# Attention into experts: another order for the last two tiles and the last gate, and the loads of expert 0's rows ahead of the next raw weights

## The chip, the cores and the metric

The kernel runs on one core of one Trainium2 chip. The metric is the device time of one execution in microseconds, here the median of three runs. Beside the timed runs there is one profiled execution, from which all rows of the trace come.

## The reference

Three stages follow one another, all in float32:

```
# 1. attention with a decaying state, per batch (4) and head (8), 768 steps, 48 wide
y[t]  = r[t] @ (state + outer(u*k[t], v[t]));  state = w[t][:,None]*state + outer(k[t], v[t])
# 2. a mixture of 8 experts on x of 3072 x 384: every token goes to its best expert alone
logits = x @ w_gate;  e = argmax(logits);  gate_w = softmax(logits)[e]
eom    = sigmoid(x @ w_output_gate)[e]
out[token] = gate_w * eom * (relu(x @ w1[e]) @ w2[e])        # 384 -> 1024 -> 384
# 3. a dense block on all tokens, 384 -> 2048 -> 384
h = x @ w_in;  out = (h * clip(h + 3, 0, 6) / 6) @ w_out
```

## The kernel before

**Attention.** The 3072 tokens are 24 tiles of 128 tokens (`NT`; tile i is chunk i // 4 of batch i % 4). The loop over i (line 692) loads tile i + 4, prepares tile i + 2 on VectorE, ScalarE and GpSimd, and does the matmuls of tile i on TensorE. Steps that the change moves are small functions, each of which issues to several engines in one go:

- `scores_pe(i)`: 16 matmuls into the banks s0 and s1; `scores(i)`: VectorE copies the allowed half into `A`.
- `ymm(i, tag)`: the outputs of a tile on TensorE, then a copy to `ys` on ScalarE (L506).
- `small_a(i, j)`: gate logits of tile i and a diagonal of tile j on TensorE, into bank x, then a copy `lts` on ScalarE. `small_p(lts)`: a matmul that turns them, into bank y (`lp`). `small_v`: ScalarE copies them to `L` (L548). `diag(j, ..)`: GpSimd writes the diagonal into `A`.
- the gate of a group g of tiles: `gate_1` (maximum, differences), `gate_2` (one-hot `O`, the chosen output logit `ls`, counts `c1` and `cnt` per expert) on VectorE, `gate_exp` on ScalarE, `gate_pe` (ranks within the expert, on TensorE), `gate_3` (the row index `pi`, the sum of exponentials), `gate_4` (the scale `sg`).
- `rows_pe(i, tag)`: four transposes of `ys`; `rows_id(i)`: GpSimd writes the token's number beside the row; `rows_act(i)`: ScalarE scales the row by `sg` into `xs` (L655); `scatter(i)`: GpSimd's indirect DMA writes 128 rows of `xs` to the places `pi` of `x_w` in DRAM (L662).

A PSUM tag (x, y, k, s0, s1) is one bank: a step that takes it waits until the last reader of what stood there is done. The order on each engine is the program's (the schedule is manual); a step waits for the data that it reads. The last groups hold two tiles each: G is (a, b) with a = 22 and b = 23, G - 1 is (a-2, a-1), G - 2 is (a-4, a-3). From line 777 the order of the last steps is written out by hand.

**The hand-over.** `keep_busy(n, ..)` issues n dummy matmuls of bfloat16 on TensorE (L382); 4, 18, 10 and 14 of them (`TAILB`) stand around the last rank matmuls, the sum of the counts (L837) and the flag (L857). After the flag VectorE makes the last eight low parts `wlo` of expert 0's weights (`piece_lo`, L351). A raw weight chunk (768 KB, 128 x 1536 float32) has two buffers, so `load_raw((1, 0), ..)`, the first chunk of expert 1, can be issued only when the low part (2, 3) is made.

**Experts.** Each expert has a window of rows of `x_w` (400 for expert 0). `window(0)` (L892) loads it in four pieces (128, 128, 128 and 16 rows), each after all 24 scatters; `window_t0` transposes it (L924, twelve transposes), ScalarE and VectorE split it into a high and a low part (L926, L927), and `first_h` is the first 18 matmuls (L966, L967, L971). From there `mm3` issues three matmuls for each product (L931 to L933). SyncE issues all loads except the scatters, in program order.

Of the kernel before, what the change touches and what calls it, by code (L numbers as in the profile page):

```python
# [7 lines left out]
F32 = mybir.dt.float32  # L8
F32R = mybir.dt.float32r
BF16 = mybir.dt.bfloat16  # L10
I32 = mybir.dt.int32
U32 = mybir.dt.uint32
AF = mybir.ActivationFunctionType
# [7 lines left out]
C = 128  # L21
# [193 lines left out]
def kernel(  # L215
# [273 lines left out]
    def ymm(i, tag="y"):  # L489
        d = tl[i]  # L490
        v, A, rh = d["v"], d["A"], d["rh"]
        last = i < B
        yp = ps_o.tile([PP, PR, C], F32, tag=tag, name="yp")

        for p in range(PR):
            for f, m in ((0, 64), (1, D)):
                c0 = (2 * p + f) * D
                nc.tensor.matmul(out=yp[64 * f:64 * f + m, p, :], lhsT=v[:, c0:c0 + m], rhs=A[:, f, p, :],  # L498
                                 start=(p == 0), stop=(last and p == PR - 1), skip_group_check=True)
        for p in range(PR) if not last else ():  # L500
            sb = d["sb"]
            for r0 in (0, 64):
                nc.tensor.matmul(out=yp[r0:r0 + D, p, :], lhsT=sb[r0:r0 + D, p, :], rhs=rh[r0:r0 + D, p, :],  # L503
                                 start=False, stop=(p == PR - 1), skip_group_check=True)
        ys = st.tile([PP, PR, C], F32, tag="ys", name="ys", bufs=12)
        nc.scalar.activation(out=ys, in_=yp, func=AF.Copy)  # L506
        d["ys"] = ys
# [9 lines left out]
            gof[i0 + j] = (g, j)  # L517
    gd = {g: {} for g in range(len(grp))}

    def small_a(i, j):  # L520

        lt = ps_o.tile([128, C], F32, tag="x", name="lt")
        src = [(z, x) for z, x in ((0, tl[i]["ys"] if 0 <= i < NT else None), (1, tl[j]["m"] if j < NT else None)) if x is not None]
        if not src:
            return None
        for n, (z, x) in enumerate(src):
            for p in range(PR):
                nc.tensor.matmul(out=lt[32 * p:32 * p + 32, :], lhsT=wg_sb[:, z, p, :], rhs=x[:, p, :],  # L528
                                 start=(n == 0), stop=(n == len(src) - 1))
        lts = wk.tile([128, C], F32, tag="lts", name="lts")  # L530
        nc.scalar.activation(out=lts, in_=lt, func=AF.Copy)
        return lts

    def small_p(lts):

        lp = ps_o.tile([128, 24], F32, tag="y", name="lp")
        nc.tensor.matmul(out=lp, lhsT=lts, rhs=sel, start=True, stop=True)
        return lp

    def small_v(i, j, lp):  # L540
        if 0 <= i < NT:
            g, z = gof[i]
            if z == 0:
                gd[g]["L"] = sm.tile([128, 4, 24], F32, tag="L", name="L")
            lq = gd[g]["L"][:, z, :]
        else:
            lq = wk.tile([128, 24], F32, tag="lq", name="lq")
        nc.scalar.activation(out=lq, in_=lp, func=AF.Copy)  # L548
        return (j, lq) if j < NT else None

    def diag(j, lq):
        av = lq[:, 16:24].rearrange("t (f p) -> t f p", f=2)
        A = wk.tile([128, 2, PR, C], F32, tag="A", name="A", bufs=4)
        nc.gpsimd.affine_select(out=A, in_=av.unsqueeze(3).to_broadcast([128, 2, PR, C]), pattern=[[0, 2], [0, PR], [1, C]],
                                compare_op=ALU.is_equal, fill=0.0, base=0, channel_multiplier=-1)
        tl[j]["A"] = A
# [6 lines left out]
    def gate_1(g):  # L563

        V = nc.vector
        d = gd[g]
        n = grp[g][1]
        lg = d["L"][:, 0:n, 0:E]
        q = gps[g % 2]
        mx, i8 = q["mx"][:, 0:n], q["i8"].rearrange("t (j e) -> t j e", e=E)[:, 0:n]  # L570
        d["df"] = sm.tile([128, 4, E], F32, tag="df", name="df")[:, 0:n]
        d["m8"] = sm.tile([128, 4], F32, tag="m8", name="m8")[:, 0:n]
        V.tensor_reduce(out=mx, in_=lg, axis=AX.X, op=ALU.max)
        V.tensor_tensor(out=d["df"], in0=lg, in1=mx.unsqueeze(2).to_broadcast([128, n, E]), op=ALU.subtract)
        V.scalar_tensor_tensor(out=i8, in0=d["df"], scalar=0.0, in1=rev8.unsqueeze(1).to_broadcast([128, n, E]),
                               op0=ALU.is_equal, op1=ALU.mult)
        V.tensor_reduce(out=d["m8"], in_=i8, axis=AX.X, op=ALU.max)
# [16 lines left out]
    def gate_exp(g):  # L594
        d = gd[g]
        n = grp[g][1]
        d["ex"] = sm.tile([128, 4, E], F32, tag="ex", name="ex")[:, 0:n]
        d["e2"] = sm.tile([128, 4], F32, tag="e2", name="e2")[:, 0:n]
        nc.scalar.activation(out=d["ex"], in_=d["df"], func=AF.Exp)
        nc.scalar.activation(out=d["e2"], in_=d["ls"], func=AF.Exp, scale=-1.0)  # L600

    def gate_pe(g, tag="y"):

        i0, n = grp[g]
        ob = gd[g]["O"]
        rk = ps_o.tile([128, 4, E], F32, tag=tag, name="rk")
        co = cnt[g % 3]
        nc.tensor.matmul(out=rk[:, 0:n], lhsT=ones_b, rhs=co.unsqueeze(1).to_broadcast([128, n, E]), start=True, stop=False)
        nc.tensor.matmul(out=rk[:, 0:n], lhsT=tri, rhs=ob, start=False, stop=(n == 1))
        for j in range(n - 1):  # L610
            nc.tensor.matmul(out=rk[:, j + 1:n], lhsT=ones_b,
                             rhs=ob[:, j:j + 1].to_broadcast([128, n - 1 - j, E]), start=False, stop=(j == n - 2))
        gd[g]["rk"] = rk
# [14 lines left out]
    def gate_4(g):  # L628

        V = nc.vector  # L630
        d = gd[g]
        n = grp[g][1]
        sx = gps[g % 2]["sx"][:, 0:n]
        d["sg"] = sm.tile([128, 4], F32, tag="sg", name="sg", bufs=4)
        V.tensor_scalar(out=sx, in0=sx, scalar1=1e-9, scalar2=None, op0=ALU.add)
        V.scalar_tensor_tensor(out=sx, in0=d["e2"], scalar=1.0, in1=sx, op0=ALU.add, op1=ALU.mult)
        V.reciprocal(out=d["sg"][:, 0:n], in_=sx)

    def rows_pe(i, tag="x"):
        xp = ps_o.tile([128, PR, 128], F32, tag=tag, name="xp")  # L640
# [18 lines left out]
    def scatter(i):  # L659

        g, j = gof[i]
        ins = nc.gpsimd.indirect_dma_start(  # L662
            out=x_w, out_offset=bass.IndirectOffsetOnAxis(ap=gd[g]["pi"][:, j:j + 1], axis=0),
            in_=tl[i]["xs"], in_offset=None)
        apart(ins, scat)
# [106 lines left out]
    def rows_to(j, tag):  # L772
        rows_pe(j, tag)
        rows_id(j)
        rows_act(j)

    scores(a)
    while sq:
        scatter(sq.pop(0))
    ymm(a - 1)  # L780
    gate_1(G - 2)
    gate_2(G - 2)
    lts = small_a(a - 2, b)
    rows_to(a - 6, "k")
    diag(*small_v(a - 2, b, small_p(lts)))
    gate_exp(G - 2)
    scatter(a - 6)
    lts = small_a(a - 1, NT)
    gate_pe(G - 2)
    gate_3(G - 2)  # L790
    gate_4(G - 2)
    rows_to(a - 5, "k")
    scatter(a - 5)
    scores(b)
    small_v(a - 1, NT, small_p(lts))
    rows_to(a - 4, "k")
    scatter(a - 4)
    ymm(a)
    gate_1(G - 1)
    gate_2(G - 1)  # L800
    gate_exp(G - 1)
    gate_pe(G - 1, "k")
    gate_3(G - 1)
    gate_4(G - 1)
    ymm(b, "s0")
    lts = small_a(a, NT)
    rows_to(a - 3, "k")
    scatter(a - 3)
    small_v(a, NT, small_p(lts))
    rows_to(a - 2, "s1")  # L810
    scatter(a - 2)
    lts = small_a(b, NT)
    rows_to(a - 1, "k")
    small_v(b, NT, small_p(lts))
    scatter(a - 1)
    gate_1(G)
    gate_2(G)
    gate_exp(G)
    rows_pe(a, "s1")
    rows_pe(b, "k")  # L820
    keep_busy(TAILB[0], ps_o, "x")
    gate_pe(G)
    gate_3(G)
    gate_4(G)
    for j in (a, b):
        rows_id(j)
    for j in (a, b):
# [34 lines left out]
    nc.vector.tensor_scalar(out=usual, in0=flag_f, scalar1=0.0, scalar2=None, op0=ALU.is_equal)  # L862
    for q, r in los:
        piece_lo((0, q), r)
        if (q, r) == (2, 3):
            load_raw((1, 0), w12[1, 0])
    keep_busy(TAILB[3], ps_o, "x")
    ph.close()

# [16 lines left out]
    def window(e):  # L886
        t = xw_p.tile([128, 4, DM], F32, tag="xw", name="xw")
        full, rest = divmod(WINS[e], 128)
        for j0, n, q in [(j, 1, 128) for j in range(full)] + [(full, 1, rest)] if e == 0 else [(0, full, 128), (full, 1, rest)]:
            if q == 0:  # L890
                continue
            ins = nc.sync.dma_start(t[0:q, j0:j0 + n, :],  # L892
                                    x_w[e * N + 128 * j0:e * N + 128 * j0 + q * n, 0:DM].rearrange("(j p) d -> p j d", j=n))
            for q in scat:
                tc.add_manual_dep(ins.ins, q.ins.name, SYNC, reason="rows of the windows")
        xw[e] = t
# [192 lines left out]
        gs[blk, f] = (hi, lo)  # L1089

    window(0)
    window_t0()
    window(1)
    f64_prefetch()
# [185 lines left out]
```

## Time and profile before

| | |
|---|---|
| median of 3 runs | 818.94 us (818.75, 818.94, 822.12) |
| profiled execution | 813.9 us, span 812.1 us |
| mean granted TensorE clock | 0.987 |
| TensorE busy | 777.2 us, 96% of the span |
| VectorE, ScalarE, GpSimd busy | 476.7, 372.7, 152.6 us |
| DMA | 85.48 MB, mean 105 GB/s |

The span runs from the first to the last instruction on the core; what the execution takes beyond it lies around them. Times within the trace count from the span's start. A granted clock of 1.00 is TensorE's 2.4 GHz, 0.50 is 1.2 GHz. "Idle before" an instruction is the time in which its engine had nothing to run, with what ended the wait behind the arrow.

### The profile page before, as it was taken

Reading aid. Unit: us, or ns where it says so; the run is one execution under the profiler, and the core shown is the slowest. Engines: PE = TensorE matmul, PEld = TensorE weight load, DVE = VectorE, ACT = ScalarE, POOL = GpSimd, SP = SyncE. Lnnn points to the kernel's source line nnn. Section 1 sums busy time; section 2 is a strip of 40 time slices with the busy share of each in tenths; the row PEclk is TensorE's granted clock in tenths of the full one; section 3 lists DMA queues with packets and bytes.
Section 4 is the critical chain, followed back from the end, with each engine's and each line's share of the span. In section 5 each row is a group of like instructions: output and inputs, shape, how many; then the busy total and the mean of one; then the engine's idle time right before and its main releaser. Section 6 shows DMA issues by size and latency. Waiting matters only on the chain.

```text
span 812.1 us, 13820 instructions
## 1 busy us (share of the span) xinstructions
PE 777.2 (96%) x5385; PEld 695.2 (86%) x5397; DVE 476.7 (59%) x946; ACT 372.7 (46%) x794; POOL 152.6 (19%) x237
## 2 busy tenths in 40 slices
PE   6999998979999999998999999999999999999996
PEld 3777776759999989998898999999999999999995
DVE  7998999536678668778776533433433343343332
ACT  4766777414554455445544433433333333333331
POOL 5777888610000000000000020020001002002002
PEclk8999999979999999999999999999999999999998
DMA  9999773143676676674511010010001001001001
GB/s 220 309 293 232 203 222 118 70 159 142 200 188 228 178 223 224 195 163 125 187 40 40 1 40 1 0 40 1 1 1 39 1 1 40 1 0 40 1 1 43
DMA packets 31868, 85.48 MB, mean 105 GB/s; under 512 B 6521, under 2 KB 17985, under 8 KB 31793
## 3 DMA queue, kind: packets, MB, share of 16 engines
q1 hardware_dynamic: 28721, 75.05, 31.7%
q0 software_dynamic: 3072, 9.45, 3.2%
q8 instruction: 44, 0.72, 0.4%
q14 instruction: 31, 0.25, 0.1%
HBM read 67.11 MB, written 17.39 MB: 104 GB/s over the span
## 4 chain that ended last, share of the span: by engine, by line
issue 40%; PE 37%; DVE 8%; DMA 7%; POOL 3%; ACT 3%; SPq 0%; POOLq 0%; ACTq 0%; DVEq 0%
DMA raw<-in_w_dram 4%; PE hp L931 4%; PE hp L932 3%; PE hp L933 3%; POOL out_dram L1166 3%; PE yp L498 3%; DVE wlo L351 3%; PE sc L452 2%; PE yp L503 2%; PE yp L933 2%; PE yp L932 2%; PE yp L931 2%; PE lt L528 2%; PE wp L382 1%; PE op L933 1%
## 5 line engine op out<-in xcount | busy, mean ns | idle before, releaser
L1082 DVE SCALAR_TENSOR_TENSOR t<-t,hp 128x512 f32<-128x512 f32 x96 | 66.0, 688 | 160.9 <-ACT t L1081 160.8
L1166 POOL DMA_INDIRECT out_dram<-ob,ids_sb x24 | 24.7, 1030 | 612.6 <-ACT ob L1164 608.0
L1081 ACT ACTIVATE t<-hp,b 128x512 f32<-128x512 f32 x96 | 65.9, 686 | 160.8 <-PE hp L933 150.2
L931 PE MATMUL op<-whi,hhi 128*128 128x384 f32 x380 | 128.4, 338 | 0.0
L932 PE MATMUL op<-wlo,hhi 128*128 128x384 f32 x380 | 128.3, 338 | 0.0
L933 PE MATMUL op<-whi,hlo 128*128 128x384 f32 x380 | 128.1, 337 | 0.0
L932 PE MATMUL hp<-xlo,win_hi 128*128 128x512 f32 x288 | 113.8, 395 | 0.4 <-DVE xlo L1070 0.4
L931 PE MATMUL hp<-xhi,win_hi 128*128 128x512 f32 x288 | 112.7, 391 | 0.9 <-ACT xhi L1069 0.9
L933 PE MATMUL hp<-xhi,win_lo 128*128 128x512 f32 x288 | 112.8, 392 | 0.0
L1088 DVE TENSOR_TENSOR hlo<-t,hhi 128x512 fp32r<-128x512 f32 x95 | 65.8, 693 | 66.3 <-ACT hhi L1087 66.3
L1087 ACT ACTIVATE hhi<-t 128x512 fp32r<-128x512 f32 x95 | 60.0, 632 | 72.2 <-DVE t L1082 72.2
L931 PEld LDWEIGHTS op<-whi,hhi 128*128 128x128 f32 x380 | 71.3, 188 | 4.1
L932 PEld LDWEIGHTS op<-wlo,hhi 128*128 128x128 f32 x380 | 71.2, 187 | 3.7
L351 DVE TENSOR_TENSOR wlo<-raw,whi 128x384 fp32r<-128x384 f32 x144 | 74.3, 557 | 0.0
L327 ACT ACTIVATE whi<-raw 128x768 fp32r<-128x768 f32 x64 | 53.9, 842 | 40.2 <-DMA raw<-in_w_dram 24.8
L933 PEld LDWEIGHTS op<-whi,hlo 128*128 128x128 f32 x380 | 71.2, 187 | 0.1
L931 PE MATMUL yp<-hhi,whi 128*128 128x360 f32 (+6 forms) x192 | 65.1, 339 | 2.7 <-ACT yst L1115 2.7
L931 PE MATMUL hp<-xhi,whi 128*128 128x360 f32 (+6 forms) x186 | 65.0, 350 | 0.9 <-ACT xhi L910 0.9
L932 PE MATMUL yp<-hlo,whi 128*128 128x360 f32 (+6 forms) x192 | 65.1, 339 | 0.2 <-DVE hlo L953 0.2
L933 PE MATMUL yp<-hhi,wlo 128*128 128x360 f32 (+6 forms) x192 | 65.0, 339 | 0.0
L933 PEld LDWEIGHTS hp<-xhi,win_lo 128*128 128x128 f32 x288 | 54.1, 188 | 11.8
L932 PE MATMUL hp<-xlo,whi 128*128 128x360 f32 (+6 forms) x186 | 63.1, 339 | 0.9 <-DVE xlo L911 0.9
(171 smaller groups left out, 1402.5 us busy)
## 6 DMA issues: line engine op xcount, KB each, us to landing
raw<-in_w_dram SPq DMA_DIRECT2D x32, 768.0 KB
a<-in_att_dram SPq DMA_DIRECT2D x23, 675.5 KB
raw<-in_wout_dram SPq DMA_DIRECT2D x16, 384.0 KB
raw<-in_win_dram SPq DMA_DIRECT2D x16, 384.0 KB
v<-in_tok_dram SPq DMA_DIRECT2D x24, 192.0 KB
wo_d<-v SPq DMA_DIRECT2D x16, 192.0 KB
raw<-wo_d SPq DMA_DIRECT2D x4, 768.0 KB
xw<-x_w SPq DMA_DIRECT2D x4, 576.0 KB
```

The lines of the kernel that those rows point to most:

```text
L327: nc.scalar.activation(out=chunks[key][0][:, sl], in_=raws[key][:, sl], func=AF.Copy)
L351: nc.vector.tensor_tensor(out=lo[:, sl], in0=raws[key][:, sl], in1=hi[:, sl].bitcast(F32), op=ALU.subtract)
L452: nc.tensor.matmul(out=scs[hf][:, p, :], lhsT=kh[r0:r0 + D, p, :], rhs=rh[r0:r0 + D, p, :], start=True, stop=True)
L498: nc.tensor.matmul(out=yp[64 * f:64 * f + m, p, :], lhsT=v[:, c0:c0 + m], rhs=A[:, f, p, :], start=(p == 0), stop=(last and p == PR - 1), ...
L931: nc.tensor.matmul(out=out_ap, lhsT=lh, rhs=rh, start=first, stop=False)
L932: nc.tensor.matmul(out=out_ap, lhsT=lh, rhs=rl, start=False, stop=False)
L933: nc.tensor.matmul(out=out_ap, lhsT=ll, rhs=rh, start=False, stop=last)
L1081: nc.scalar.activation(out=t, in_=hp, func=AF.Relu, bias=b_3)
L1082: nc.vector.scalar_tensor_tensor(out=t, in0=t, scalar=6.0, in1=hp, op0=ALU.min, op1=ALU.mult)
L1087: nc.scalar.activation(out=hi, in_=t, func=AF.Copy)
L1088: nc.vector.tensor_tensor(out=lo, in0=t, in1=hi.bitcast(F32), op=ALU.subtract)
L1166: ins = nc.gpsimd.indirect_dma_start(out=out, out_offset=bass.IndirectOffsetOnAxis(ap=ids_sb[:, i:i + 1], axis=0), in_=ob, in_offset=None)
```

## The change

Four things are changed. The hand-written order of the last tiles is another one, with other banks: `scores_pe(b)`, `ymm(a)` and `ymm(b)` come earlier among their neighbours, `gate_pe(G - 1)` stands behind `ymm(b)`, and the scatters of a-2 and a-1 stand behind the last `small_v`. The last gate is a function of its own, `gate_last`, in which the sum of exponentials comes from the exponential's own accumulator on ScalarE, and the scale `sg` is made ahead of the index `pi` and of the counts. `load_raw((1, 0))` is issued after `window(0)` instead of in the midst of the low parts. And the second and fourth piece of `window(0)` are issued by ScalarE's queue.

```diff
-    def small_a(i, j):
+    def small_a(i, j, tag="x"):
...
-    def small_p(lts):
+    def small_p(lts, tag="y"):
...
+    def gate_last(g):
+        gate_1(g)
...
+        for j in range(n):
+            nc.scalar.activation(out=ex[:, j], in_=d["df"][:, j], func=AF.Exp, accum_out=sa[:, j:j + 1])
+        V.tensor_tensor(out=d["O"], in0=i8, in1=d["m8"].unsqueeze(2).to_broadcast([128, n, E]), op=ALU.is_equal)
+        keep_busy(TAILB[0], ps_o, "x")
+        gate_pe(g)
+        V.tensor_tensor(out=lo, in0=d["L"][:, 0:n, E:2 * E], in1=d["O"], op=ALU.mult)
+        V.tensor_reduce(out=ls, in_=lo, axis=AX.X, op=ALU.add)
+        nc.scalar.activation(out=e2, in_=ls, func=AF.Exp, scale=-1.0)
+        V.tensor_scalar(out=sx, in0=sa, scalar1=1e-9, scalar2=None, op0=ALU.add)
+        V.tensor_tensor(out=pb, in0=d["rk"][:, 0:n], in1=d["O"], op=ALU.mult)
+        V.tensor_reduce(out=pf, in_=pb, axis=AX.X, op=ALU.add)
+        V.scalar_tensor_tensor(out=sx, in0=e2, scalar=1.0, in1=sx, op0=ALU.add, op1=ALU.mult)
+        V.reciprocal(out=d["sg"][:, 0:n], in_=sx)
+        V.tensor_scalar(out=d["pi"][:, 0:n], in0=pf, scalar1=float(E * N - 1), scalar2=None, op0=ALU.min)
+        V.tensor_reduce(out=q["c1"], in_=d["O"].rearrange("p j e -> p e j"), axis=AX.X, op=ALU.add)
+        V.tensor_tensor(out=cnt[(g + 1) % 3], in0=q["c1"], in1=cnt[g % 3], op=ALU.add)
...
     ymm(a - 1)
+    lts = small_a(a - 2, b)
     gate_1(G - 2)
     gate_2(G - 2)
-    lts = small_a(a - 2, b)
-    rows_to(a - 6, "k")
-    diag(*small_v(a - 2, b, small_p(lts)))
     gate_exp(G - 2)
-    scatter(a - 6)
-    lts = small_a(a - 1, NT)
-    gate_pe(G - 2)
+    scores_pe(b)
+    lts_1 = small_a(a - 1, NT, "k")
+    diag(*small_v(a - 2, b, small_p(lts, "x")))
+    small_v(a - 1, NT, small_p(lts_1, "k"))
+    gate_pe(G - 2, "x")
     gate_3(G - 2)
     gate_4(G - 2)
-    rows_to(a - 5, "k")
+    rows_to(a - 6, "k")
+    scatter(a - 6)
+    ymm(a)
+    rows_to(a - 5, "x")
     scatter(a - 5)
     scores(b)
-    small_v(a - 1, NT, small_p(lts))
-    rows_to(a - 4, "k")
-    scatter(a - 4)
-    ymm(a)
+    lts = small_a(a, NT, "k")
     gate_1(G - 1)
     gate_2(G - 1)
     gate_exp(G - 1)
-    gate_pe(G - 1, "k")
+    rows_to(a - 4, "x")
+    scatter(a - 4)
+    ymm(b, "s0")
+    gate_pe(G - 1, "x")
     gate_3(G - 1)
     gate_4(G - 1)
-    ymm(b, "s0")
-    lts = small_a(a, NT)
-    rows_to(a - 3, "k")
+    small_v(a, NT, small_p(lts, "k"))
+    rows_to(a - 3, "s1")
     scatter(a - 3)
-    small_v(a, NT, small_p(lts))
-    rows_to(a - 2, "s1")
+    lts = small_a(b, NT, "x")
+    rows_pe(a - 2, "k")
+    small_v(b, NT, small_p(lts, "y"))
+    rows_id(a - 2)
+    rows_act(a - 2)
     scatter(a - 2)
-    lts = small_a(b, NT)
-    rows_to(a - 1, "k")
-    small_v(b, NT, small_p(lts))
+    rows_to(a - 1, "s1")
     scatter(a - 1)
-    gate_1(G)
-    gate_2(G)
-    gate_exp(G)
-    rows_pe(a, "s1")
+    rows_pe(a, "s0")
     rows_pe(b, "k")
-    keep_busy(TAILB[0], ps_o, "x")
-    gate_pe(G)
-    gate_3(G)
-    gate_4(G)
+    gate_last(G)
...
     for q, r in los:
         piece_lo((0, q), r)
-        if (q, r) == (2, 3):
-            load_raw((1, 0), w12[1, 0])
...
-            ins = nc.sync.dma_start(t[0:q, j0:j0 + n, :],
+            ins = (nc.scalar if e == 0 and j0 % 2 else nc.sync).dma_start(t[0:q, j0:j0 + n, :],
...
     window(0)
+    load_raw((1, 0), w12[1, 0])
     window_t0()
```

## Rows read from the trace of the kernel before

**Rows 1.** The page: TensorE's busy time, and its granted clock in 40 slices.

```profile
PE 777.2 (96%) x5385; PEld 695.2 (86%) x5397; DVE 476.7 (59%) x946; ACT 372.7 (46%) x794; POOL 152.6 (19%) x237
...

```

**Rows 2.** Windows: length, busy PE, PEld, DVE, ACT, POOL, granted clock, DMA share, GB/s.

```profile
168.00:169.00 1.00, 1.00 (x7) 0.46 (x5) 1.00 (x4) 0.00 (x0) 0.00 (x0) 1.00 0.00 0
...
170.00:170.90 0.90, 0.61 (x3) 0.20 (x2) 0.90 (x3) 0.00 (x0) 0.00 (x0) 1.00 0.00 0
170.90:172.00 1.10, 0.00 (x0) 0.00 (x0) 0.90 (x3) 0.00 (x0) 0.00 (x0) 1.00 0.75 179
172.00:173.00 1.00, 0.00 (x0) 0.00 (x0) 0.00 (x0) 0.00 (x0) 0.00 (x0) 0.93 0.93 387
...
175.00:176.00 1.00, 1.00 (x5) 1.00 (x6) 0.00 (x0) 0.00 (x0) 0.00 (x0) 0.50 0.20 69
...
183.20:184.00 0.80, 0.80 (x6) 0.80 (x5) 0.11 (x1) 0.61 (x2) 0.00 (x0) 1.00 1.02 419
...
200.00:800.00 600.00, 594.01 (x3111) 550.80 (x3110) 318.91 (x590) 252.63 (x429) 22.63 (x40) 1.00 0.25 76
```

**Rows 3.** Chain that ended last, 159 to 186 us: start, us, what.

```profile
169.98 0.33 SPq L319
170.62 4.18 DMA xw<-x_w
174.93 2.49 PE xp L924 x11
177.46 0.51 ACT xhi L926
178.02 0.70 PE hp L966
...
183.85 0.18 PE hp L931
```

**Rows 4.** Timeline of TensorE: start, us, instruction, idle before.

```profile
148.50 0.40 PE L537 MATMUL lp<-sel,lts 128*128 128x24 f32 x2 [0.90 <-ACT lts L531]
...
167.64 2.97 PE L382 MATMUL wp<-busy,ones_b 128*128 128x512 bf16 x13
```

**Rows 5.** Waits of SyncE's queue, 138 to 186: us, times, longest.

```profile
SPq L319 <- DVE wlo L351: 37.1, 1, 37.1
```

**Rows 6.** Timeline of GpSimd: the last two scatters.

```profile
164.53 0.98 POOL L662 DMA_INDIRECT x_w<-xs,pi  x1 [1.53 <-ACT xs L655]
...
165.82 0.96 POOL L662 DMA_INDIRECT x_w<-xs,pi  x1 [0.21 <-POOL gap L291]
```

**Rows 7.** Line L662, all scatters: from issue to landing.

```profile
DMA to landing us min/median/max: 2.6/2.7/6.0
```

**Rows 8.** Timeline of ScalarE: last weight pieces, and the first half of expert 1's.

```profile
164.13 1.75 ACT L346 ACTIVATE whi<-raw 128x384 fp32r<-128x384 f32 x4
...
190.19 0.85 ACT L327 ACTIVATE whi<-raw 128x768 fp32r<-128x768 f32 x1 [0.87 <-PE yp L932]
```

**Rows 9.** Timeline of VectorE in the last gate.

```profile
161.17 0.18 DVE L591 TENSOR_REDUCE vps<-O 128x8 f32<-128x16 bf16 x1
161.39 0.17 DVE L592 TENSOR_TENSOR cnt<-vps,cnt 128x8 bf16<-128x8 f32 x1
...
162.85 0.17 DVE L637 RECIPROCAL sg<-vps 128x2 f32<-128x2 f32 x1
```

**Rows 10.** Groups by line: reading an accumulator (busy us, mean ns).

```profile
L442 ACT ACTIVATION_READ_ACCUMULATOR junk<-R,b_lo 112x1 f32 x24 | 4.6, 190 | 0.0
```

**Rows 11.** Chain that ended last, 130 to 200: four transposes of expert 1's rows.

```profile
193.58 0.52 PE xp L909 x4
```

**Rows 12.** Timeline of TensorE and ScalarE around `ymm(a)`.

```profile
152.69 1.08 PE L503 MATMUL yp<-rh,sb 48*48 48x128 f32 x16
...
155.10 0.60 ACT L506 ACTIVATE ys<-yp 112x512 f32<-112x512 f32 x1 [2.53 <-PE rk L611]
```

More of the change, by code (lines that the diff above doesn't have):

```diff
@@ L518 @@
     gd = {g: {} for g in range(len(grp))}
-    def small_a(i, j):
-        lt = ps_o.tile([128, C], F32, tag="x", name="lt")
+    def small_a(i, j, tag="x"):
+        lt = ps_o.tile([128, C], F32, tag=tag, name="lt")
         src = [(z, x) for z, x in ((0, tl[i]["ys"] if 0 <= i < NT else None), (1, tl[j]["m"] if j < NT else None)) if x is not None]
@@ L532, in small_a @@
         return lts
-    def small_p(lts):
-        lp = ps_o.tile([128, 24], F32, tag="y", name="lp")
+    def small_p(lts, tag="y"):
+        lp = ps_o.tile([128, 24], F32, tag=tag, name="lp")
         nc.tensor.matmul(out=lp, lhsT=lts, rhs=sel, start=True, stop=True)
@@ L637, in gate_4 @@
         V.reciprocal(out=d["sg"][:, 0:n], in_=sx)
+    def gate_last(g):
+        V = nc.vector
+        d = gd[g]
+        n = grp[g][1]
+        gate_1(g)
+        q = gps[g % 2]
+        i8, lo = (q[x].rearrange("t (j e) -> t j e", e=E)[:, 0:n] for x in ("i8", "lo"))
+        pf, sx = (q[x][:, 0:n] for x in ("pf", "sx"))
+        d["O"] = sm.tile([128, 4, E], BF16, tag="O", name="O")[:, 0:n]
+        ls = sm.tile([128, 4], F32, tag="ls", name="ls")[:, 0:n]
+        ex = sm.tile([128, 4, E], F32, tag="ex", name="ex")[:, 0:n]
+        sa = sm.tile([128, 4], F32, tag="sa", name="sa", bufs=1)[:, 0:n]
+        e2 = sm.tile([128, 4], F32, tag="e2", name="e2")[:, 0:n]
+        pb = sm.tile([128, 4, E], F32, tag="pb", name="pb")[:, 0:n]
+        d["pi"] = sm.tile([128, 4], I32, tag="pi", name="pi", bufs=4)
+        d["sg"] = sm.tile([128, 4], F32, tag="sg", name="sg", bufs=4)
+        for j in range(n):
[14 more added lines that the diff above has]
+        V.tensor_tensor(out=cnt[(g + 1) % 3], in0=q["c1"], in1=cnt[g % 3], op=ALU.add)
     def rows_pe(i, tag="x"):
```

## The prediction

> **What bounds the kernel now.** I read the page first. TensorE is busy for 96% of the span, and the granted clock is at 0.9 or more in all but three of forty slices [rows 1]. So after the attention stage only TensorE's time counts. The windows by stage say it sharply: from 200 to 800 us TensorE is busy 594.0 of 600 us at full clock, and DMA has a quarter of its share in use [rows 2]. The change touches nothing there. Whatever moves the moment at which expert 0 reaches its steady rhythm should move the end by as much.
>
> The second view is the chain of work that ended last, at the hand-over from attention to experts [rows 3]. There it leaves TensorE: SyncE issues raw weights (169.98), then the load of expert 0's rows (`xw`, 170.62, 4.18 us) is in flight; the transposes start at 174.93, `first_h` runs from 178.02 to 183.85, and from there one matmul follows the other at 0.18 us. The reader should see two slow things in it. TensorE has nothing to do between its last dummy matmul (167.64 + 2.97 = 170.61 [rows 4]) and 174.93: 4.3 us. And what follows runs at half clock: the 0.93 of 172 to 173 says that the granted clock fell from 1.00 to 0.50 at 172.9, 2.3 us into the idle time, and it is full again only by 183.2 [rows 2].
>
> The third view, SyncE's waits, says why the load is late. Its queue is in order, and `load_raw((1, 0))` stands ahead of the window's loads. It waits for VectorE's `wlo` (L351), which frees its buffer, and was held there 37.1 us [rows 5], until 169.98. The last scatter, which the loads really need, was issued at 165.82 [rows 6] and landed 2.7 us after [rows 7]: 168.5. So the loads stood ready for 2.1 us behind another transfer's wait, and then had its 768 KB in front of them as well.
>
> **The change part by part.**
>
> *Loads ahead of the raw weights, on two queues.* What leaves the path is SyncE's wait for L351 and the raw issue. From the last landing I allow 0.3 us to the first issue, as between the end of the raw issue (169.98 + 0.33 = 170.31) and 170.62 [rows 3]. The raw issue began at 169.98 and nothing moved until 170.9 [rows 2]: 1.0 us to the first bytes. The first two blocks are 384 KB, and at the 387 GB/s of 172 to 173 us [rows 2] that is 1.0 us. For the completion I allow 0.5 us, an estimate: from 168 the windows show no scatter packets, and the landing is at 168.5. Sum from the landing: 0.3 + 1.0 + 1.0 + 0.5 = 2.8 us to what the first transposes need, so 171.3 if the last scatter stays where it was. Two issues on each queue instead of four on one save two issues of 0.33 us or a little more [rows 3], which lies inside the last two blocks' time. ScalarE has nothing else to do there: it ends its weight pieces at 164.13 + 1.75 = 165.9 [rows 8] and next runs at 177.46 [rows 3]. No row shows ScalarE's queue issuing a load. Its bounds are no more than SyncE's, and as much as the 4.2 us that `xw` took behind 768 KB [rows 3]; I take the low end, since the case is nearest to SyncE's own issues with nothing in front.
>
> *The raw weights behind.* They still wait for L351's fourth piece, so they are issued near 170.2, about when they were, with the rows already in flight. They are needed at 190.19 by the first half of `whi` [rows 8], some 20 us later; with all the rest moved up by 7 us that still leaves some 12 us of cover for 2.0 us of transfer (768 KB at 387 GB/s). If the cover went, that 0.85 us piece would be late, and TensorE would notice at expert 1. I cost it at nothing.
>
> *The final gate.* In `gate_last` the two class counts (L591, L592), the sum of exponentials (L625) and the integer index (L626) no longer stand before `sg`. They are four VectorE steps of about 0.2 us from one start to the next (161.17, 161.39 [rows 9]): 0.8 us off the 162.85 at which `sg` begins. The sum comes from ScalarE instead: two exponentials of some 0.2 us and two accumulator reads of 0.19 us [rows 10], 0.8 us where there was one exponential. They are hidden while VectorE still works on the one-hot and the logit; if ScalarE first has rows to scale, they come 0.6 us late and eat most of the gain.
>
> *The order of the last tiles.* Nothing is added or taken away: the same matmuls, transposes, gates, scatters. TensorE has little idle time to win there, 0.9 us in front of one `lp` [rows 4]. Walking through the new order, `ymm(a)` moves ahead of two row transposes, and those of a-1 move behind the last `small_p`. I get the last logits some 0.7 us earlier (0.9 idle and 0.55 of transposes less, 0.75 more for hand-overs through ScalarE in banks x and k). The last rank matmul I leave where it was, since now three tiles of transposes and four dummies stand between it and the logits, before two tiles and four. So the scatters come some 0.8 us earlier (bounds 0 and 1.6), the last landing is at 167.7, and the rows could be there at 170.5.
>
> *What starts the transposes, then.* The dummies: 18, 10 and 14 follow the last rank matmul in TensorE's order and end at 170.6 as before (bounds 170.0 and 172.0, by how that matmul moves). With rows at 170.5 to 171.3 and dummies at 170.6 the transposes begin at 171.0. **Gained: 174.93 - 171.0 = 3.9 us** (bounds 2.9 and 4.4).
>
> *The clock.* TensorE would now stand still for under half a microsecond, where before it stood for 2.3 us until the clock fell. At full clock four of the later transposes take 0.52 us [rows 11], so twelve take 1.56 where 174.93 to 177.46 [rows 3] are 2.53: **0.97 us.** The 0.56 us from their end to the first matmul (177.46 to 178.02, ScalarE's `xhi`) stay. `first_h` has 18 matmuls of 400 columns in 178.02 to 183.85, 5.83 us; the next ones, of the same width, are 0.18 us apart [rows 3], so 18 take 3.26: **2.57 us.** The bounds of both terms are nothing and this.
>
> Sum: 3.9 + 0.97 + 2.57 = **7.4 us**. The profiled execution took 813.9 us around its span of 812.1, and would take 806.5; the median of the runs, 818.94, is 5 us above it, and I carry that difference over: **811.5 us.** `first_h` would end at 176.4.
>
> **A rule against it.** First the row: through the transposes the clock stayed at 1.2 GHz (0.50 from 175 to 176 [rows 2]), and it was full only by 183.2, after 5 us of `first_h`'s matmuls. That leaves open whether transposes hold it up. The Trainium skill, "TensorE: Matmul & The Clock Gate", Part 4: PE-mode transpose, says that work in transpose mode does not count as busy for the clock in the way matmuls do. By that rule TensorE would look idle from the last dummy to `first_h` and the sum would be rival 1's; no run here shows it yet.
>
> **The rivals.**
> 1. *The clock falls all the same*, during the transposes or just after. For it: from 170.6 to 173.1 there would be no matmul, as long as from 170.61 to the fall at 172.9. Against it: in attention, where transposes are mixed with matmuls, the slices stay full [rows 1]. If the transposes and `first_h` run as slowly as before, only the 3.9 us remain: 815.0. If the clock stays low into expert 0, to 183.2 as before, 10 us at half pace cost 5.1 of the 7.4: 816.6. If it catches only half of `first_h`: 812.8.
> 2. *The new order costs the tail.* `gate_pe(G - 1)` now stands behind `ymm(b)`, so the scales of a-2 and a-1 come about a microsecond later, and scatters follow each other on GpSimd at 1.3 us at best (164.53, 165.82 [rows 6]). If the last landing comes 2 us later than I say, the transposes begin near 172.8: 813.3.
> 3. *The rows are slow by themselves*: the 4.2 us of the load [rows 3] are its own and not the queue's. A landing at 168.0 + 4.2 = 172.2 saves 2.7; with the clock held 812.7, with it lost 816.2. Against it: at 387 GB/s the 4.2 us move far more than 600 KB.
> 4. *The other side: hand-overs in shared banks.* In the new order almost every step of TensorE takes bank x or k from a step that ScalarE or VectorE must have read. The row that speaks for a high price: ScalarE stood 2.53 us before `ys` of tile a and got it at 155.10, 1.3 us after its matmuls ended (152.69 + 1.08 = 153.77) [rows 12]. Ten such hand-overs at 1.2 us are 12 us: 823.5. It decides once more than six of them cost that (7.4 us). Against it: TensorE's own wait in the tail was 0.9 us [rows 4].
>
> **How the numbers follow.** Chances: as reckoned 0.70, rival 1 0.13, rival 2 0.08, rival 3 0.06, rival 4 0.03. The likeliest gives 811.5, with 810 to 813 as its own range (transposes from 170.0 to 172.5). Below 809.5 I leave 0.05 (more idle time won than I see); above 815.5 the worse half of rival 1, half of rival 3 and rival 4, some 0.12. So the range is 809.5 to 815.5. About 0.5%, 4.1 us, is what a measurement of this kernel can tell from no change: faster means below 814.8. There lie the main case, rival 2, the milder part of rival 1 and half of rival 3: 0.85. Same: 0.12. Slower: rival 4, 0.03.
>
> **What would show it.** SyncE's four `xw` issues become two, near 168, and the raw load follows near 170.2; ScalarE's queue has the other two. TensorE's wait for `xw` shrinks from 4.3 us to under 1, the transposes begin near 171.0 and are 0.13 us apart, `first_h` ends near 176.4, and the windows from 170 to 184 show a granted clock of 1.00. The last scatter starts near 165.0. From there every row is the old one, 7.4 us earlier. The prediction is wrong if the last scatter starts after 166.5, if the transposes begin after 172.5, or if the clock column shows 0.50 after 170.

## The result, and the profile after

| | before | after |
|---|---|---|
| median of the runs taken side by side (20 each) | 821.63 us | 815.07 us |
| ratio, with its 95% interval | | 0.9916 (0.9896 to 0.9937) |
| profiled execution | 813.9 us, span 812.1 | 816.7 us, span 815.0 |

The ratio is a gain of 6.9 us (5.2 to 8.5, from 821.63); 7.4 were forecast, which is a ratio of 0.991. The two medians are both some 3 us above where the three first runs of before had put the scale, so the gain is to be read from the ratio. One of the 20 runs after (823.04) was a slow one, and the ratio leaves it out.

The two profiled executions alone would say the opposite: the span after is 2.9 us longer. This is the first thing to clear up. Runs of one kernel differ by more than the gain (808 to 823 us after, 817 to 828 before), and the trace shows where: in stages that the change does not touch. The first score matmul of tile 22 (L452), which stands ahead of every edit, starts at 143.31 before and at 146.93 after: 3.6 us were lost in attention. From the first matmul behind `first_h` to the end of the span it is 628.4 us before and 634.4 after: 6.0 us more. There ScalarE waited longer for raw weights than before (24.8 us in 10 waits then), though what made the loads late is not shown:

```profile
ACT whi L327 <- DMA raw<-in_w_dram: 35.8, 12, 7.6
```

Over all thirteen profiled executions of this study that last part lies between 626.6 and 636.8 us, with the changed kernel itself at 634.4 and, taken once more, at 626.9 (with 22.1 us of such waits). So these 6.0 us need not come from the change, and I compare the **stretch** from the first score matmul of tile 22 to the first matmul behind `first_h`: 143.31 to 183.69 before, 40.4 us, and 146.93 to 180.56 after, 33.6 us. The stretch is 6.7 us shorter, what the ratio says too.

This is the chain that ended last, after, in the same place as [rows 3] (start, us, what). Line numbers of the changed kernel are higher: L953 is the transposes of `window_t0`, L955 `xhi`, L995, L996 and L1000 `first_h`, L960 to L962 are `mm3`, L921 the window's loads.

```profile
172.49 2.42 DVE wlo L351 x5
175.02 1.60 PE xp L953 x12
176.65 0.51 ACT xhi L955
177.21 0.45 PE hp L995
...
179.65 1.08 PE hp L1000 x6
180.72 0.18 PE hp L960
```

The loads are no longer a link of it. From the first transpose to ScalarE's `xhi` it takes 1.63 us (175.02 to 176.65) instead of 2.53, and `first_h` has the pace of 0.18 us from its first matmuls on. The timelines of the queues and of TensorE show how the rows came (SPq is SyncE's queue, ACTq ScalarE's):

```profile
171.96 0.88 ACTq L921 DMA_DIRECT2D xw<-x_w  x2
...
172.01 0.80 SPq L921 DMA_DIRECT2D xw<-x_w  x2
174.03 0.33 SPq L319 DMA_DIRECT2D raw<-in_w_dram  x1
```

```profile
168.92 0.97 POOL L696 DMA_INDIRECT x_w<-xs,pi  x1 [0.21 <-issue]
...
171.68 2.96 PE L382 MATMUL wp<-busy,ones_b 128*128 128x512 bf16 x13
175.02 1.58 PE L953 MATMUL xp<-ident,xw 128*128 128x128 f32 x12 [0.37 <-DVE wlo L351]
```

The last scatter starts at 168.92, the two queues issue two loads each from 172.0, the last dummy ends at 174.64, and TensorE stands still for 0.4 us where it stood for 4.3 [rows 3, 4]. (Both rows hold 13 of the 14 dummies, 2.96 and 2.97 us; where all 14 are recorded they take 3.18 us, so both waits can be 0.2 us shorter.) The releaser in brackets is a guess of the profile: the low parts were being made at the time, but the load of the first block is what ends 3.0 us after its issue, and it ended this wait in the kernels below, where the row names it. The clock holds (same columns as [rows 2]):

```profile
172.00:173.00 1.00, 1.00 (x7) 0.41 (x5) 1.00 (x5) 0.00 (x0) 0.00 (x0) 1.00 0.05 5
...
175.00:176.00 1.00, 0.98 (x8) 0.85 (x9) 0.85 (x3) 0.00 (x0) 0.00 (x0) 1.00 0.81 181
...
177.00:178.00 1.00, 0.79 (x4) 0.79 (x5) 0.81 (x2) 0.95 (x3) 0.00 (x0) 1.00 0.84 229
```

The granted clock is 1.00 in every microsecond from 158 to 191; before it was 0.50 from 172.9 to 183.1. It shows in the page's slices as well, each 20 us long: the ninth digit is 7 before and 9 after. Before:

```profile
PEclk8999999979999999999999999999999999999998
```

After:

```profile
PEclk8899999999999999999999999999999999999998
```

### The profile page after: what moved, and what is told of

Same layout as the page of the kernel before. It is cut to its first block, busy times and chain, and to the rows that moved or that the text cites. A ratio compares the mean times of both kernels' runs of the same rounds, so it can differ in the third digit from the quotient of the medians.

```text
span 815.0 us, 13821 instructions
## 1 busy us (share of the span) xinstructions
PE 780.2 (96%) x5385; PEld 695.8 (85%) x5397; DVE 477.2 (59%) x945; ACT 373.7 (46%) x797; POOL 152.7 (19%) x237
## 4 chain that ended last, share of the span: by engine, by line
issue 40%; PE 26%; DMA 14%; DVE 11%; ACT 4%; POOL 3%; SPq 0%; ACTq 0%; POOLq 0%; DVEq 0%
DMA raw<-in_w_dram 8%; DMA a<-in_att_dram 5%; DVE wlo L351 3%; POOL out_dram L1196 3%; PE hp L960 3%; PE hp L961 3%; PE hp L962 3%; PE yp L498 2%; PE sc L452 1%; PE yp L961 1%; PE yp L962 1%; PE yp L960 1%; DVE R L389 1%; PE op L962 1%; PE op L960 1%
## 5 line engine op out<-in xcount | busy, mean ns | idle before, releaser
L1196 POOL DMA_INDIRECT out_dram<-ob,ids_sb x24 | 24.8, 1034 | 612.6 <-ACT ob L1194 608.0
L960 PE MATMUL op<-whi,hhi 128*128 128x384 f32 x380 | 128.4, 338 | 0.0
L962 PE MATMUL op<-whi,hlo 128*128 128x384 f32 x380 | 128.1, 337 | 0.0
L960 PE MATMUL hp<-xhi,win_hi 128*128 128x512 f32 x288 | 113.1, 393 | 1.5 <-ACT xhi L1098 1.5
L962 PE MATMUL hp<-xhi,win_lo 128*128 128x512 f32 x288 | 113.3, 393 | 0.0
L960 PEld LDWEIGHTS op<-whi,hhi 128*128 128x128 f32 x380 | 71.3, 188 | 4.1
L962 PEld LDWEIGHTS op<-whi,hlo 128*128 128x128 f32 x380 | 71.2, 187 | 0.2 <-DVE hlo L1117 0.2
L960 PE MATMUL yp<-hhi,whi 128*128 128x360 f32 (+6 forms) x192 | 65.5, 341 | 3.5 <-ACT hhi L981 1.9
L960 PE MATMUL hp<-xhi,whi 128*128 128x360 f32 (+6 forms) x186 | 65.5, 352 | 1.6 <-ACT xhi L939 1.6
L962 PE MATMUL yp<-hhi,wlo 128*128 128x360 f32 (+6 forms) x192 | 65.2, 339 | 0.0
L962 PEld LDWEIGHTS hp<-xhi,win_lo 128*128 128x128 f32 x288 | 54.5, 189 | 11.9
```

Source lines behind the costliest of these rows:

```text
L960: nc.tensor.matmul(out=out_ap, lhsT=lh, rhs=rh, start=first, stop=False)
L962: nc.tensor.matmul(out=out_ap, lhsT=ll, rhs=rh, start=False, stop=last)
L1196: ins = nc.gpsimd.indirect_dma_start(out=out, out_offset=bass.IndirectOffsetOnAxis(ap=ids_sb[:, i:i + 1], axis=0), in_=ob, in_offset=None)
```

## The experiments

Each of the eleven kernels was run beside the kernel before, on the same chip as it. The table gives, from each profiled execution, the start of the first score matmul of tile 22, of the last gate's first rank matmul (L608), of the last scatter, of the first transpose of expert 0's rows, of the first matmul behind `first_h`, and the stretch, which is the fifth less the first. The ratios are against before.

| kernel | tile 22 | rank | last scatter | transposes | behind first_h | stretch | ratio (95%) |
|---|---|---|---|---|---|---|---|
| before | 143.31 | 160.95 | 165.82 | 174.93 | 183.69 | 40.4 | |
| after | 146.93 | 164.99 | 168.92 | 175.02 | 180.56 | 33.6 | 0.9916 (0.9896 to 0.9937) |
| loads alone | 146.02 | 163.28 | 168.15 | 174.05 | 179.52 | 33.5 | 0.9925 (0.9895 to 0.9954) |
| tail alone | 145.53 | 163.67 | 167.61 | 177.56 | 185.48 | 40.0 | 0.9987 (0.9956 to 1.0017) |
| after, no last dummies | 143.85 | 161.87 | 165.80 | 171.60 | 178.44 | 34.6 | 0.9923 (0.9894 to 0.9953) |
| before, 34 last dummies | 143.16 | 160.78 | 165.65 | 175.03 | 180.47 | 37.3 | 0.9937 (0.9908 to 0.9967) |
| loads and gate, old order | 146.80 | 163.16 | 167.17 | 173.12 | 178.55 | 31.8 | 0.9903 (0.9871 to 0.9936) |
| after, one queue | 144.82 | 161.75 | 165.68 | 171.69 | 177.41 | 32.6 | 0.9916 (0.9886 to 0.9947) |
| second queue alone | 145.29 | 161.66 | 166.53 | 175.46 | 183.61 | 38.3 | 1.0003 (0.9973 to 1.0034) |
| after, transposes as dummies | 145.96 | 162.89 | 166.82 | 173.03 | 178.45 | 32.5 | 0.9903 (0.9865 to 0.9941) |
| after, once more | 149.07 | 165.99 | 169.92 | 175.93 | 181.37 | 32.3 | 0.9924 (0.9902 to 0.9946) |
| loads and gate, 11 dummies | 146.09 | 162.45 | 166.46 | 172.31 | 177.72 | 31.6 | 0.9906 (0.9881 to 0.9932) |
| after, old gate | 143.53 | 160.46 | 165.10 | 170.96 | 176.46 | 32.9 | 0.9951 (0.9920 to 0.9982) |

One thing must be known to read it. From tile 22 to the rank matmul it is 17.3 to 18.1 us in the first six rows and 16.4 to 16.9 in the last seven, for the same instructions (the changed kernel itself: 18.06 and 16.92). The section on the hardware comes back to it. Within either set kernels with the same order of the tiles agree to 0.4 us, so I compare stretches within a set, or count from the rank matmul or the last scatter. The expectations for the second set were written with numbers of the first: four of its stretches (one queue, second queue alone, transposes, loads and gate) lie 0.7 to 1.0 us below the range expected for them. The intervals of the ratios are some 0.3% (2.5 us) to either side: they tell the kernels with a gain from those with none, and the parts of the gain are told apart by the traces alone, one execution of each kernel.

**Loads alone.** Which half of the change carries the gain?

```diff
     for q, r in los:
         piece_lo((0, q), r)
-        if (q, r) == (2, 3):
-            load_raw((1, 0), w12[1, 0])
...
-            ins = nc.sync.dma_start(t[0:q, j0:j0 + n, :],
+            ins = (nc.scalar if e == 0 and j0 % 2 else nc.sync).dma_start(t[0:q, j0:j0 + n, :],
...
     window(0)
+    load_raw((1, 0), w12[1, 0])
```

> The kernel before with the second half of the change alone: raw weights (1, 0) issued after the window's loads, and two of these on ScalarE's queue; the old order of the tiles and the old last gate. Measured from the first score matmul of tile 22 to the end of first_h, the stretch was 40.5 us before and is 33.8 us after the change. Theory (the loads carry the gain): the last scatter stays where it was, the rows land some 0.5 us later than with the whole change, the clock holds: stretch 34 to 35 us, the end 5.5 to 6.5 us below before. Rival (the clock falls, since TensorE now stands still for more than 1 us after its dummies): stretch 37 to 38.5 us, gain 2 to 3.5 us. Rival (the tail carries the gain): stretch 38 us or more.

The stretch is 33.5 us, the changed kernel's own, and half a microsecond less than I expected. TensorE waits for the rows and says so:

```profile
169.98 2.97 PE L382 MATMUL wp<-busy,ones_b 128*128 128x512 bf16 x13
174.05 1.51 PE L922 MATMUL xp<-ident,xw 128*128 128x128 f32 x12 [1.10 <-DMA xw<-x_w]
```

It stands still for 1.1 us, the transposes start when they do in the changed kernel (28.0 us after tile 22, there 28.1), and the clock stays up. The loads carry the whole gain.

**Tail alone.** The other half: the new order and `gate_last`, with the raw weights ahead of the window's loads and SyncE issuing all of them.

> The first half of the change alone: the new order of the last tiles and gate_last, with the raw weights ahead of the window's loads and all of these on SyncE as before. Theory: the loads wait for the raw weights and these for the low parts, which follow the dummies and so the last rank matmul; that was 0.4 us later in the changed kernel, so the stretch is 40.5 to 41.2 us (40.5 before) and the end within 1 us of before. Rival (the tail is worth something by itself, since the last scatter is 0.5 us earlier): stretch 40.0 us or less, the end 0.5 us or more below.

The last scatter starts 3.9 us after the rank matmul instead of 4.9, but nothing comes of it, as SyncE is still held by the low parts: the raw weights go out at 172.71, and TensorE waits for the rows as it did.

```profile
177.56 2.58 PE L955 MATMUL xp<-ident,xw 128*128 128x128 f32 x12 [4.23 <-DMA xw<-x_w]
```

The transposes start 32.0 us after tile 22, 0.4 later than before, because the dummies follow the rank matmul and the low parts the dummies. That the stretch comes out at 40.0 all the same, where the rival had it, is the clock's doing and not the tail's: it fell at 177.1 and was back at 183.9, 3.2 us into the matmuls of `first_h`.

```profile
177.00:178.00 1.00, 0.44 (x2) 0.47 (x3) 0.00 (x0) 0.00 (x0) 0.00 (x0) 0.53 1.00 369
...
183.00:184.00 1.00, 1.00 (x5) 0.99 (x4) 0.00 (x0) 0.00 (x0) 0.00 (x0) 0.55 1.14 376
```

The time is that of before within its interval.

**The changed kernel without its last dummies.** The rows are early, but TensorE stands still until they come.

```diff
-TAILB = (4, 18, 10, 14)
+TAILB = (4, 18, 10, 0)
...
+    if TAILB[3]:
-    keep_busy(TAILB[3], ps_o, "x")
+        keep_busy(TAILB[3], ps_o, "x")
```

> The changed kernel without the last 14 dummy matmuls: TensorE stands still from some 171.7 (in the changed kernel's time) until the rows are there, about 3.3 us. Theory (the clock is a term of its own): the granted clock falls to 0.50 there, the transposes start when they did, and they and first_h cost up to 3.5 us more: stretch 36.5 to 37.5 us against 33.8, the end 3 to 4 us above the changed kernel. Rival (only the earlier load counts): stretch 33.5 to 34.2 us, the end as the changed kernel's.

Between the two: 34.6 us, 1.0 more than with the dummies. The row of the transposes and the windows show why not 3.5.

```profile
171.60 1.54 PE L954 MATMUL xp<-ident,xw 128*128 128x128 f32 x12 [3.08 <-DMA xw<-x_w]
```

```profile
169.00:170.00 1.00, 0.00 (x0) 0.00 (x0) 1.00 (x3) 0.00 (x0) 0.00 (x0) 1.00 0.36 77
...
172.00:173.00 1.00, 1.00 (x11) 0.73 (x8) 0.73 (x3) 0.00 (x0) 0.00 (x0) 1.00 0.60 184
173.00:174.00 1.00, 0.39 (x4) 0.29 (x3) 0.27 (x1) 0.80 (x3) 0.00 (x0) 0.63 1.03 424
...
176.00:177.00 1.00, 1.00 (x6) 1.00 (x5) 0.00 (x0) 0.00 (x0) 0.00 (x0) 0.67 1.10 393
177.00:178.00 1.00, 1.00 (x7) 1.00 (x7) 0.00 (x0) 0.00 (x0) 0.00 (x0) 1.00 1.05 310
```

TensorE stood still for 3.1 us, the transposes still ran at full clock, and it fell only at 173.3 and was back by 176.7: 3.4 us low, where it had been low for 10.2 before. The clock is a term of its own, but its price depends on when it falls. In the timed runs this kernel is not to be told from the changed one.

**The kernel before with 34 dummies in place of the last 14.** The late loads stay, the clock is held.

> The kernel before with 34 dummy matmuls in place of the last 14, so that TensorE stays busy until the late rows arrive; nothing else is changed. Theory (the clock's 3.5 us are had without any earlier load): the transposes still start 4.3 us after the old dummies' end, at full clock, stretch 36.8 to 37.5 us against 40.5, the end 3 to 4 us below before. Rival (the clock does not matter, or transposes let it fall): stretch 39.5 us or more, the end within 1 us of before.

The transposes start 0.05 us behind the last dummy, at the old place, and at full clock:

```profile
167.48 7.50 PE L382 MATMUL wp<-busy,ones_b 128*128 128x512 bf16 x33
175.03 1.49 PE L924 MATMUL xp<-ident,xw 128*128 128x128 f32 x12
```

The stretch is 37.3 us, 3.1 below before: in the traces nearly half of the whole gain comes from 20 more dummy matmuls, without any transfer being earlier. The time is 0.63% below, 5.2 us (2.7 to 7.5), where I expected 3 to 4. This pulls the two terms of the sum apart with the loads late; with the loads early the kernel above puts the clock's term at 1.0 us only.

**Transposes as dummies.** The changed kernel with its last 14 dummies replaced by 23 transposes, so that between the flag's matmul and `first_h` TensorE does nothing but transpose.

```diff
-    keep_busy(TAILB[3], ps_o, "x")
+    wp = ps_o.tile([128, 512], F32, tag="x", name="wp")
+    for _ in range(23):
+        nc.tensor.transpose(out=wp[:, 0:128], in_=ident, identity=ident)
```

> The changed kernel with its last 14 dummy matmuls replaced by 23 transposes, which keep TensorE as long, so that between the flag's matmul and first_h there is no matmul for some 5.7 us but TensorE hardly stands still. Theory A (transposes do not hold the clock): the granted clock falls to 0.50 before or in first_h, as it did 2.3 us after the last dummy in the kernel before; stretch 35 us or more. Theory B (they hold it as matmuls do): the clock stays at 1.00, stretch 33.4 to 34.0 us.

The timeline of TensorE, and the windows of the same stretch:

```profile
169.37 0.17 PE L888 MATMUL fp<-fb,ones_b 128*128 128x1 bf16 x1
169.59 2.73 PE L898 MATMUL wp<-ident 128*128 128x128 f32 x23
173.03 1.46 PE L955 MATMUL xp<-ident,xw 128*128 128x128 f32 x12 [0.71 <-DMA xw<-x_w]
175.10 0.46 PE L997 MATMUL hp<-xhi,whi 128*128 128x400 f32 x1 [0.61 <-ACT xhi L957]
```

```profile
171.00:172.00 1.00, 1.00 (x12) 1.00 (x10) 1.00 (x3) 0.00 (x0) 0.00 (x0) 1.00 0.83 252
172.00:173.00 1.00, 0.32 (x3) 0.08 (x1) 1.00 (x3) 0.00 (x0) 0.00 (x0) 1.00 1.19 378
...
174.00:175.00 1.00, 0.49 (x5) 0.26 (x3) 0.00 (x0) 0.46 (x2) 0.00 (x0) 1.00 1.00 418
...
178.00:179.00 1.00, 1.00 (x8) 1.00 (x7) 0.35 (x1) 0.85 (x2) 0.00 (x0) 1.00 1.04 341
```

For 5.5 us (169.59 to 175.10) there is no matmul but transposes, with 1.3 us of standing still among them, and the clock is 1.00 throughout. When TensorE stood still altogether it fell 2.3 us after its last matmul (before), 3.7 (tail alone) and 4.1 (second queue alone), and, with 3.1 us of standing still and then transposes, 4.7 (no last dummies). So here transposes held the clock up: theory B, in one execution, in which 5.5 us is 0.8 us more than the longest of the four. The ratio can't say it of the timed ones, since the kernel whose clock fell at 173.3 (no last dummies) has nearly the same.

**One queue, and the second queue alone.** What is ScalarE's queue worth? The first kernel is the changed one with all loads on SyncE, the second the kernel before with two of the four on ScalarE, and the raw weights still ahead of the others.

> The changed kernel with all four loads of the window on SyncE's queue. Theory (the order of the transfers is what counts, the second queue saves only two issues of 0.4 us): the first transposes start as early or a little earlier, the last pieces come up to 0.9 us later, stretch 33.6 to 34.6 us against 33.6. Rival (the second queue carries a good part): stretch 35 us or more.

> The kernel before with the second and fourth load of the window on ScalarE's queue, the raw weights still ahead of the other two on SyncE's. Theory (the order counts): the first 128 rows still wait for the raw weights, the transposes start within 1 us of where they did (31.6 us after the first score matmul of tile 22), stretch 39 to 40.5 us against 40.4. Rival: transposes at 30 us or earlier, stretch 38 us or less.

With one queue the transposes start 6.0 us after the last scatter, with two 6.1 (after) and 6.0 (after, once more). With one queue and in the latter they follow the last dummy within 0.1 us, so these starts don't say when the first rows came. What shows is that they take 1.77 us instead of 1.49 to 1.58, as the last pieces come later, and that the stretch is 0.3 us above that of the changed kernel taken once more in the same set (32.6 and 32.3). The second queue alone brings nothing: ScalarE's two loads go out early, SyncE's first one still stands behind the raw weights.

```profile
169.35 0.83 ACTq L892 DMA_DIRECT2D xw<-x_w  x2
```

```profile
175.46 2.47 PE L924 MATMUL xp<-ident,xw 128*128 128x128 f32 x12 [3.92 <-DMA xw<-x_w]
```

```profile
175.00:176.00 1.00, 0.54 (x3) 0.57 (x4) 0.00 (x0) 0.00 (x0) 0.00 (x0) 0.79 0.17 63
```

Of the 2.1 us by which its stretch of 38.3 us lies below that of before, 1.3 belong to the second set; from the rank matmul the transposes start after 13.8 us, before after 14.0, and 0.6 come from the clock, which fell later (175.6).

**The tail taken apart.** The old order with `gate_last` and the loads; the changed kernel with the old gate; and the changed kernel once more.

> The old order of the tiles with gate_last and the loads' half of the change. The loads alone had the last scatter 22.1 us and the transposes 28.0 us after the first score matmul of tile 22, with 1.1 us of idle TensorE in front of them, and a stretch of 33.5 us. Theory (gate_last is worth its 0.8 us where ScalarE has no rows to scale first, and the new order of the tiles gives that away): last scatter at 21.2 to 21.5, transposes at 27.0 to 27.4, stretch 32.6 to 33.0 us. Rival (gate_last is worth nothing): last scatter at 22 or later, stretch 33.4 to 33.8 us.

> The changed kernel with the old last gate (gate_1, gate_2, gate_exp, dummies, gate_pe, gate_3, gate_4) in the new order of the tiles. Theory (gate_last is worth 0.4 to 0.9 us on the last scatter, the order costs 0.5 us): last scatter 4.4 to 4.9 us after gate_pe(G) against 3.9 with gate_last, transposes 0.3 to 0.9 us later than the changed kernel's in this call, clock held. Rival (in the new order ScalarE's rows hide all that gate_last saves): last scatter 3.9 to 4.1 us after gate_pe(G), stretch within 0.2 us of the changed kernel's.

> The changed kernel itself, beside the two that follow. From earlier runs: gate_pe(G) 16.9 to 18.1 us after the first score matmul of tile 22, whatever the kernel by 1.1 us between chips; last scatter 3.9 us after gate_pe(G); stretch 32.5 to 33.7 us; 0.7 to 1.1% below before.

From the rank matmul to the last scatter it takes 4.87 us with old gate and old order (four kernels), 4.01 with `gate_last` alone, 4.64 with the new order alone, 3.93 with both. `gate_last` saves 0.86 us in the old order and 0.71 in the new one. The rank matmul itself comes later in the new order in both sets: 18.0 to 18.1 us after tile 22 against 17.3 to 17.6, and 16.9 against 16.4. So the order costs some 0.5 us on the rank matmul, and the old order with `gate_last` has the earliest last scatter: 20.4 us after tile 22, the changed kernel 20.9 in the same set. Its stretch is 31.8 us against 32.3. The timed ratios are too wide to tell these apart.

**Fewer dummies.** In that kernel the transposes followed the last dummy at once. Do the dummies hold them up?

```diff
-TAILB = (4, 18, 10, 14)
+TAILB = (4, 18, 10, 11)
```

> The old order of the tiles, gate_last, the loads' half of the change, and 11 dummies in place of the last 14 (0.65 us less). With 14 the transposes started 0.08 us after the last dummy. Theory (rows and dummies end together there, so that nothing more is to be had): transposes 0.1 to 0.4 us earlier against the last scatter than with 14 dummies (5.95 us after it), idle TensorE in front of them; stretch 0.8 to 1.2 us below the changed kernel's in this call, the end 0 to 0.3% below it. Rival (the dummies alone set the start): the transposes start 0.6 us earlier.

```profile
169.15 2.53 PE L382 MATMUL wp<-busy,ones_b 128*128 128x512 bf16 x11
172.31 1.46 PE L950 MATMUL xp<-ident,xw 128*128 128x128 f32 x12 [0.63 <-DMA xw<-x_w]
```

The dummies end 0.65 us earlier, the transposes start 0.10 earlier against the last scatter, and TensorE waits 0.63 us for the rows. It is the shortest stretch of all (31.6 us), 0.7 us below the changed kernel's in the same set (I expected 0.8 to 1.2); all but 0.1 of that is there with 14 dummies already (31.8). Its ratio, taken beside the changed kernel's, is 0.9906 against 0.9924; the intervals overlap, so it is better by nothing that the timing shows.

## Why the prediction was right, point by point

- **The bound.** Right: the stretch is shorter by 6.7 us and the ratio says 6.9 (5.2 to 8.5); what is won at the hand-over arrives at the end. What the traces can't exclude is a loss of a microsecond or two in the expert stage, whose length differs by 10 us from one execution to the next. As a time, 815.07 us lies just inside the stated range (809.5 to 815.5) and outside the main case's own (810 to 813), because before was itself at 821.63 and not at 818.94; 0.9916 of 818.94 is 812.1.
- **The raw weights behind.** Costed at nothing, rightly for the load that was moved: it is issued at 174.03, and the first half of expert 1's `whi` waits for TensorE and not for it.

```profile
187.06 0.85 ACT L327 ACTIVATE whi<-raw 128x768 fp32r<-128x768 f32 x1 [0.88 <-PE yp L961]
```

- **The transposes' start.** Forecast 3.9 us earlier, measured 3.5 against tile 22 (31.6 to 28.1). The signs of being wrong were given in the time of the span before; less the 3.6 us that attention took longer, the last scatter starts at 165.3 and the transposes at 171.4, both inside their limits (166.5 and 172.5). The mechanism was right: SyncE's wait for the low parts was the brake, as the loads alone show. The term that was too small is the rows' load. I allowed 2.8 us from the last landing to what the transposes need. The last scatter's 2.7 us taken from 5.85, which is what passes from its start to the transposes where these wait (fewer dummies), leaves 3.15 us. The windows suggest what most of the difference is, a slow half microsecond behind the first bytes: those of the changed kernel show 61 GB/s from 173.0 to 173.5 and only then 366.

```profile
172.50:173.00 0.50, 0.50 (x4) 0.22 (x3) 0.50 (x3) 0.00 (x0) 0.00 (x0) 1.00 0.10 9
173.00:173.50 0.50, 0.50 (x4) 0.26 (x3) 0.50 (x3) 0.00 (x0) 0.00 (x0) 1.00 0.52 61
173.50:174.00 0.50, 0.50 (x4) 0.20 (x3) 0.50 (x2) 0.00 (x0) 0.00 (x0) 1.00 0.98 366
```

- **The clock.** Forecast 0.97 + 2.57 = 3.5 us, measured 5.54 instead of 8.76 from the first transpose to the first matmul behind `first_h`: 3.2. The kernel before with more dummies gets 3.1 without earlier loads. The term was a little too large, mainly because the end of `first_h` was read from the chain (183.85); in TensorE's timeline the matmul behind it starts at 183.69, so its 18 matmuls took 5.67 us, and after 3.35 (177.21 to 180.56). That the size fits owes something to the one execution: in the two other profiles with late loads and no added dummies the same part took 7.92 and 8.15 us, and there the clock had only 2.4 and 2.6 us to give back.
- **The rule against it** (the Trainium skill, "TensorE: Matmul & The Clock Gate", Part 4: PE-mode transpose). Taken as a rule about a clock that is already up it does not hold here: 5.5 us without a matmul other than transposes, at 1.00. Whether transposes could raise a low clock no run shows; in the kernel before they ran at 0.50 from beginning to end. The clock of 1.00 after puts rival 1 out by a measurement.
- **The tail.** The forecast was 0.8 us on the last scatter and a rank matmul that stays. Measured against tile 22: the last scatter 0.5 us earlier (22.5 to 22.0), the rank matmul 0.4 later (0.4 and 0.55 in the second set). `gate_last` gives what was reckoned, 0.7 to 0.9. The walk through the order was wrong: I had the last logits 0.7 us earlier, so that a third tile of transposes behind them would leave the rank matmul where it was. Their last matmul (`lp`) starts 15.6 us after tile 22 before and after, and the rank matmul then comes 2.5 us after it instead of 2.0. `gate_last` more than made up for that.
- **Rivals 2 to 4.** The last scatter starts 0.3 us later than forecast and not 2, so rival 2 is out: the order costs the tail 0.4 us and not two. Rival 3: the rows take 3.0 us from issue to use instead of 4.3 with 768 KB in front, so most but not all of that time was their own. Rival 4 exists in small: two hand-overs of about a microsecond (below), far from six, and before has as many.

## What to carry to other kernels

In a queue that is in order, look at what the transfer ahead waits for: here 768 KB that were needed 20 us later held back 600 KB that everything waited for. When a stall on the critical engine is removed, price the clock behind it as well: of 6.7 us, 3.2 were work at half speed after the wait, and in the traces dummy matmuls alone get that part. And when the profiled executions of two kernels differ by more than the change can explain, take a stretch that begins ahead of the first edit and ends behind the last one.

## What the runs showed of the hardware that was not expected

**A hand-over from TensorE can take a microsecond more in one execution than in another.** The same two instructions of the changed kernel, first in its first profile, then in its second: the last matmuls of `ymm(b)` and ScalarE's copy of their result.

```profile
158.92 1.08 PE L503 MATMUL yp<-rh,sb 48*48 48x128 f32 x16
...
161.00 0.60 ACT L506 ACTIVATE ys<-yp 112x512 f32<-112x512 f32 x1 [2.36 <-PE xp L677]
```

```profile
160.79 1.08 PE L503 MATMUL yp<-rh,sb 48*48 48x128 f32 x16
...
161.92 0.60 ACT L506 ACTIVATE ys<-yp 112x512 f32<-112x512 f32 x1 [1.41 <-PE yp L503]
```

In the first, ScalarE starts 1.0 us after the matmuls end by the profile (158.92 + 1.08 = 160.00), in the second 0.05 us after. Before had the longer one at `ymm(a)` [rows 12]. In the first, TensorE waits for that copy as well:

```profile
161.65 0.43 PE L528 MATMUL lt<-ys,wg_sb 112*32 112x128 f32 x8 [0.83 <-ACT ys L506]
```

With a second slow one at `ymm(a-1)`, which costs 0.3 us, this is the 1.1 us by which the two sets of the table differ. Each profile of the first six rows has two such hand-overs (0.8 to 1.3 us) between the scores of tile 22 and the rank matmul, and none of the last seven has one (0.04 to 0.05 us each). It is not the kernel, then, nor the chip, as I supposed in an expectation above: the loads alone (17.3 us to the rank matmul) and the fewer dummies (16.4) were taken on the same one. The ends of matmuls are modelled, so the rows don't say whether TensorE or the signal is late; what makes it come and go is open.

**The clock fell between 2.3 and 4.7 us after the last matmul ahead of the wait**, in four executions with 3.1 to 4.3 us of idle time, and stayed low for 3.4 to 10.2 us. From the first transpose to the first matmul behind `first_h` these four took 6.8 to 8.8 us, the kernels that kept the clock 5.4 to 5.7: much the same wait cost between 1.3 and 3.2 us behind it. They are four kernels with one profile each, so whether one and the same program varies as much is not shown.
